# A new hand-written order for the opening of a fused attention and max-out kernel, with one load for the first states

## The chip, the cores and the metric

The kernel runs on one core of one Trainium2 chip. Its metric is the device time of one execution in microseconds; three runs gave 149.94, 150.06 and 150.39 us, so the median is 150.06 us. Lower is better.

## What is computed

Eight batches with eight heads each; x is a sequence of 512 rows of 64, and `state` has 32 rows of 64 for each batch and head. x reads the states by a softmax, the states read x by another, and all rows of both readings, with the heads side by side (512 wide), go through a max-out layer.

```python
scores = scale * x @ state.T          # per batch and head; scale = 1/8
xread  = softmax(scores)  @ state     # 512 rows
sread  = softmax(scores.T) @ x        # 32 rows
rows   = concat([xread, sread])       # (8 * 544) rows of 512
out    = maximum(rows @ w1, rows @ w2) @ w_out     # w1, w2: 512x1024, w_out: 1024x512
```

All inputs and the output are float32 in the chip's main memory.

## The kernel before, in words

**The algebra.** max(h1, h2) is relu(h1 - h2) + h2. So the kernel forms wd = w1 - w2 (512x1024) and wwo = w2 @ w_out (512x512) once, and a batch needs relu(rows @ wd) @ w_out + rows @ wwo. Since xread is a softmax times the state, state @ wd and state @ wwo are made first for each batch (`sw`, 32 rows for each head), and the softmax weights are multiplied with those (`l1` for the relu part, the `o` part of `l2` for the other). The eight heads stand as two groups g of four heads of 32 rows each, 128 rows in all.

**The stages of a batch.** x is loaded as two halves of four heads (512 KB each, `load_x`), cast to bfloat16 (`cast_e` four pieces, `cast_b` two pieces) and transposed: for batches 0 and 1 on TensorE (`xt`, evicted by `xte`), for the others by a transposing DMA (`xtd`). `sc` makes the scores against `sbd`, a tile with the transposed states (two half batches hh), `exp` evicts them on ScalarE, `red` sums and inverts on VectorE, `mul` normalises, and the weights are transposed (`at` on TensorE and its eviction `ate` for batches 0 and 1, `atd` by DMA for the others). `sw` (L331 on, eight products to a token) and its evictions `swe`; `l1` with the evictions `re` (a relu, on ScalarE or VectorE); `l2` with the evictions `le`; then `store`. The other reading, `sr`, is made directly for batches from 2 on; for batches 0 and 1 `srw` makes a wider product, `swre` evicts it into `srx`, and `srp` (`sr_pick`, four copies of 32 partitions each) later picks out the right parts. `srx` lies in the same memory as batch 2's `sw` tile, so `swe.2` waits for the picks.

**The weights.** Each of w1, w2 and w_out comes in four pieces of 512 KB (`ldw1`, `ldw2`, `ldwo`). For w1 and w2, pieces 0 and 1 are the columns 0 to 511 (rows 0 to 255 and 256 to 511) and pieces 2 and 3 the columns 512 to 1023. Each piece of w2 is cast (`cw2`), transposed on TensorE (`w2`) and evicted (`w2e`) for wwo; each piece of w_out is cast (`cwo`); `ww.i.q` adds to row block i of wwo what a quarter q of the 1024 columns gives, and `wwe` evicts it. `sub.k.h` makes half h of piece k of wd from the float32 pieces of w1 and w2. `sw.b.0` and `sw.b.1` need the columns 0 to 511 and 512 to 1023 of wd, `sw.b.w` needs wwo.

**The order.** Batches 0 and 1 and the start of batch 2 run by ORDER, a list of tokens that a loop (L517) emits in turn; every engine does its own tokens in that order, and waits are placed by the tile framework. A token is name.arguments@PSUM banks>engine (A ScalarE, V VectorE, P GpSimd); `fill.k@bank` is a product of zeros on TensorE that nothing reads (512 columns where k is 100 or more, else 256). SyncE issues the loads, transposes and stores in the order of the list. The states come by `ldS.lo.hi` (L178): 0 in ScalarE's DMA queue, 1 and then 2 to 7 in SyncE's; `cS` casts states 0 and 1, `S` transposes them on TensorE, `Se` evicts one half j of the partitions into `sbd`. States 2 to 7 are cast with a mask in two parts (`mS`, L202) and transposed into `sbd` by one DMA (`Sd`, L211).

**The rest.** From batch 2 on a plain loop (L602) does l1 of batch b, scores of b + 1, casts and transposes of b + 2, the load of b + 3, then l2 of b; RELEASE tells in which order its banks come. A sum check (`check_sums`) ends in a product with a column of ones whose result, `flag` (L645, L646), decides whether a general path runs. The last batch and the state rows (`m1`, `m2`) follow. WHOLE names batches whose x comes as one load of 1 MB (L621).

## Time and profile before

| What | Value |
|---|---|
| median of three runs | 150.06 us |
| the profiled execution's own time | 150.39 us |
| span of that execution, first to last instruction | 148.5 us |
| TensorE busy | 138.9 us (94%), 1185 products |
| VectorE, ScalarE, GpSimd busy | 84.7, 67.3, 55.7 us |
| mean granted TensorE clock | 0.996 |
| main memory read, written | 15.20 MB, 8.91 MB |

The profile is of one execution. Times in its rows are microseconds from the first instruction. PE is TensorE (PEld its weight loads), DVE VectorE, ACT ScalarE, POOL GpSimd, SP SyncE; a q behind a name is that engine's sequencer, which issues DMAs. L336 is line 336 of the kernel. Rows of the chain of waits give start, length and what; rows of the timeline give start, length, engine, line, operation, written tile <- read tile, shape and count, and in brackets how long the engine stood idle before it and what ended that. The length of a product on TensorE is that of one product from its start to its modelled end; products overlap, and the chain gives the pace. In rows on DMA issues the last number is the time from issue to landing, in us.

### The profile page before, as it was taken

How to read it: one execution, taken by the hardware profiler on the slowest of the kernel's cores; microseconds unless marked ns; L12 is line 12 of the kernel's file. 1: busy time of each engine (PE TensorE's matmuls, PEld its weight loads, DVE VectorE, ACT ScalarE, POOL GpSimd, SP SyncE). 2: the span in 40 equal slices, each digit the busy share in tenths (PEclk: the TensorE clock that was granted, in tenths of full speed). 3: DMA queues.
4: the chain of work that ended last, by engine and by line, in shares of the span. 5: the costliest groups of instructions: out<-in, count | busy, mean ns of one | idle time of the engine just before them, and what ended most of it. 6: DMA issues, size and time to landing. Idle time of an engine off the chain costs nothing.

```text
span 148.5 us, 3021 instructions
## 1 busy us (share of the span) xinstructions
PE 138.9 (94%) x1185; PEld 69.2 (47%) x1185; DVE 84.7 (57%) x164; ACT 67.3 (45%) x123; POOL 55.7 (38%) x89
## 2 busy tenths in 40 slices
...
GB/s 136 309 376 388 384 387 382 281 281 226 83 203 76 72 185 382 282 187 328 249 93 274 256 181 102 252 306 122 71 71 216 29 44 177 110 0 131 81 160 61
DMA packets 36063, 29.44 MB, mean 198 GB/s; under 512 B 23120, under 2 KB 31568, under 8 KB 35152
## 3 DMA queue, kind: packets, MB, share of 16 engines
...
q8 instruction: 10, 0.16, 0.5%
...
HBM read 15.20 MB, written 8.91 MB: 162 GB/s over the span
## 4 chain that ended last, share of the span: by engine, by line
PE 83%; DMA 11%; SPq 1%; DVE 1%; issue 0%; ACT 0%
PE bank L373 37%; PE bank L359 19%; PE bank L368 10%; DMA big<-in_moe_w_dram 8%; PE bank L336 4%; DMA big<-in_x_dram 3%; PE bank L488 3%; PE bank L392 2%; PE bank L402 2%; PE bank L248 2%; PE bank L288 1%; PE bank L400 1%; DVE wd L444 1%; SPq L175 1%; PE bank L432 1%; SPq L171 0%
## 5 line engine op out<-in xcount | busy, mean ns | idle before, releaser
L373 PE MATMUL bank<-wo,r 128*128 128x512 bf16 (+1 forms) x264 | 60.8, 373 | 0.0
L373 PEld LDWEIGHTS <-r 128*128 128x128 bf16 x264 | 25.5, 98 | 28.9 <-issue 0.2
L354 DVE TENSOR_SCALAR r<-bank 128x512 bf16<-128x512 f32 x30 | 20.7, 691 | 19.5 <-PE bank L359 19.1
L359 PE MATMUL bank<-at,sw 128*128 128x512 bf16 x128 | 30.1, 379 | 0.0
L101 ACT COPY big<-bank 128x512 f32<-128x512 f32 (+1 forms) x17 | 9.7, 573 | 41.3 <-PE bank L373 39.7
L264 POOL TENSOR_TENSOR a<-e,er 128x512 bf16<-128x512 bf16 x15 | 15.9, 1079 | 29.9 <-DVE er L261 15.0
L352 ACT ACTIVATE r<-bank 128x512 bf16<-128x512 f32 x34 | 20.4, 609 | 6.6 <-PE bank L359 6.5
L103 DVE CAST sw<-bank 128x512 bf16<-128x512 f32 x24 | 15.1, 684 | 7.2 <-PE bank L336 6.5
L368 PE MATMUL bank<-sw,at 128*128 128x512 bf16 (+1 forms) x66 | 19.0, 374 | 0.0
L103 DVE COPY big<-bank 128x512 f32<-128x512 f32 (+1 forms) x16 | 10.6, 661 | 14.5 <-PE bank L373 14.5
L359 PEld LDWEIGHTS <-sw 128*128 128x128 bf16 x128 | 12.1, 98 | 13.8 <-DVE sw L103 0.3
L105 POOL CAST xb<-big 128x1024 bf16<-128x1024 f32 x12 | 12.3, 1039 | 15.7 <-DMA big<-in_x_dram 10.8
L105 POOL CAST xe<-big 128x512 bf16<-128x512 f32 x26 | 15.3, 622 | 6.3 <-DMA big<-in_x_dram 6.3
L101 ACT CAST sw<-bank 128x512 bf16<-128x512 f32 x24 | 12.7, 599 | 3.2 <-PE bank L336 3.1
L256 ACT ACTIVATE e<-bank 128x512 bf16<-128x512 f32 x16 | 8.9, 594 | 9.5 <-PE bank L248 9.0
L260 DVE TENSOR_REDUCE sums<-e 128x16 f32<-128x512 bf16 x16 | 10.5, 656 | 3.1 <-ACT e L256 3.0
L488 PE MATMUL bank<-wo,w2m 128*128 128x512 bf16 x32 | 8.1, 379 | 0.4 <-POOL wo L105 0.3
L368 PEld LDWEIGHTS <-at 128*128 128x128 bf16 x66 | 5.5, 98 | 5.0 <-issue 0.2
L454 PE MATMUL bank<-wz 128*128 128x512 bf16 (+1 forms) x18 | 5.5, 422 | 1.3 <-DVE ones L457 1.3
L248 PEld LDWEIGHTS <-xt 128*128 128x128 bf16 x128 | 5.1, 98 | 1.9
L336 PE MATMUL bank<-wd,sbd 64*32 64x512 bf16 x128 | 5.7, 382 | 0.1
L248 PE MATMUL bank<-sbd,xt 128*128 128x64 bf16 x128 | 5.5, 193 | 0.0
...
## 6 DMA issues: line engine op xcount, KB each, us to landing
...
big<-in_moe_w_dram SPq DMA_DIRECT2D x8, 512.0 KB, 11.3
big<-in_moe_w_out_dram SPq DMA_DIRECT2D x4, 512.0 KB, 10.8
...
sf<-in_state_dram SPq DMA_DIRECT2D x1, 384.0 KB, 11.1
```

Source lines behind the costliest of these rows:

```text
L101: nc.scalar.copy(o, i)
L103: nc.vector.tensor_copy(o, i)
L105: nc.gpsimd.tensor_copy(o, i)
L248: nc.tensor.matmul(pv[:, c, kk], xt_s[b % 2][:, c, k, :], sbd[:, b, k, :], start=(c == 0 and kk == 0), stop=(c == NC - 1 and kk == 1))
L264: (nc.gpsimd if eng == "P" else nc.vector).tensor_mul(e_view(a_s[b % 2], hh), e_view(e_s[b % 2], hh), er_s[b % 2][:, hh].unsqueeze(3).to_b ...
L336: nc.tensor.matmul(pg[g][32 * i:32 * i + 32, 0:n], sbd[64 * g:64 * g + 64, b, i, 32 * g:32 * g + 32], rhs, start=True, stop=True)
L352: nc.scalar.activation(out=o, in_=p, func=ACTF.Relu)
L354: nc.vector.tensor_scalar(o, p, scalar1=0.0, scalar2=None, op0=ALU.max)
L359: nc.tensor.matmul(p, sw_s[b % 3][:, g, f * 128:(f + 1) * 128], at_s[b % 3][:, g].rearrange("p c t -> p (c t)"), start=(g == 0), stop=(g = ...
L368: nc.tensor.matmul(p[:, lo:hi], at_s[b % 3][:, g, c, :], sw_s[b % 3][:, g, FF + lo:FF + hi], start=(start and g == 0), stop=(stop and g == 1))
L373: nc.tensor.matmul(p[:, lo:hi], r_s[b % 2][:, f, c * 128:(c + 1) * 128], wo[:, f, lo:hi], start=(start and j == 0), stop=(stop and j == le ...
L488: nc.tensor.matmul(p, w2t[:, f, i, :], wo[:, f, :], start=(first and f % 2 == 0), stop=(last and f % 2 == 1))
```

## The change

It replaces ORDER, with the same work in it but for the fills (27 in place of 18) and the states: one load `ldS.0.2` in ScalarE's queue brings states 0 and 1, two neighbouring rows of a state to a partition (pieces of 512 bytes in place of 256), `cS.0.2` casts both, `S.0.2` transposes both, and `Se` makes two copies, each of which puts the row pairs back in order. The list has other weight pieces first (columns 512 to 1023 ahead of columns 0 to 511), another choice of engine for several evictions and casts, both `mS` on ScalarE, both halves of batch 2's x ahead of the load of states 2 to 7, and `srp` ahead of `mul.2.0` where it stood behind both `mul.2`. RELEASE changes. x of batch 7 comes in two loads. The product of `flag` has 128 columns of ones (`full`, set by GpSimd behind the list) where it had two. `gate` is defined and the new list doesn't call it. The old list is shown down to its first l1, the new one in full.

```diff
--- before.py
+++ after.py
@@ -21,37 +21,37 @@
 ORDER = """
-ldx.0.0 ldS.0.1 fill.113@0 ldx.0.1 fill.104@1 ldS.1.2 fill.112@0 ldx.1.1 fill.111@1 ldx.1.0 fill.108@0 fill.13@1
-ldw2.0 fill.109@0 ldw2.1 fill.115@1 fill.105@0 ldwo.0 ce.0.0>V ce.0.1>A fill.11@1 ldw1.1 cS.0.1>V xt.0.0@1 ldwo.1
-S.0.1@0 ldw1.0 fill.0@2 ce.0.2>V ce.0.3>A ldw2.3 Se.0.1.0>V cS.1.2>P Se.0.1.1>V xte.0.0>A xt.0.1@2 ldw2.2 fill.15@0
-S.1.2@3 xte.0.1>V Se.1.2.1>A sc.0.0@1 ldwo.3 ce.1.2>P Se.1.2.0>A fill.102@0 sc.0.1@2 exp.0.0>A fill.2@0 fill.12@3
-ce.1.3>V ldwo.2 exp.0.1>A red.0.0>V xt.1.1@1 srw.0@2,3 ce.1.0>A ce.1.1>P red.0.1>V ldw1.2 mul.0.0>P xte.1.1>A xt.1.0@0
-swre.0.1>V mul.0.1>P cw2.0>A ldw1.3 xte.1.0>V swre.0.0>V cw2.1>P at.0.0@0 sc.1.0@2 ldx.3.1 w2.0@3 ate.0.0>V exp.1.0>A
-fill.114@0 sc.1.1@1 w2e.0>V cwo.0>P w2.1@0 exp.1.1>A at.0.1@2 red.1.0>V w2e.1>A ww.1.0@1 srw.1@3,4 red.1.1>V sub.1.1>P
-ldS.2.8 ww.3.0@0 mul.1.1>V cwo.1>A fill.1@5 fill.3@6 ww.2.0@7 sub.1.0>V swre.1.0>A ww.0.1@6 sub.0.0>V swre.1.1>A
-ww.1.1@1 ww.3.1@0 sub.0.1>V ww.0.0@6 ate.0.1>V mul.1.0>P sw.0.0@4,3 sw.1.0@2,5 swe.0.0.1>A swe.0.0.0>V ww.2.1@7
-cw2.3>P swe.1.0.1>A at.1.1@3 swe.1.0.0>V l1.0.2@4 at.1.0@5 ate.1.1>V cw2.2>P w2.3@2 re.0.2>A ate.1.0>V l1.0.3@3
...
+ldx.0.0 ldS.0.2 fill.10@0 ldx.0.1 fill.109@1 ldx.1.1 fill.114@0 fill.11@1 ldx.1.0 fill.110@0 ldw2.2 fill.100@1
+fill.9@0 ldw2.3 fill.111@1 ldwo.2 fill.0@0 fill.5@1 fill.101@0 ldw1.3 ce.0.1>A ce.0.0>V ldwo.3 xt.0.0@0 cS.0.2>V
+ldw1.2 fill.106@1 xte.0.0>V fill.105@2 ce.0.3>P ce.0.2>A ldw2.1 S.0.2@1 xt.0.1@2 ldw2.0 Se.0.2.1>A Se.0.2.0>V sc.0.0@1
+xte.0.1>V fill.13@0 ldwo.0 fill.6@3 ce.1.2>P exp.0.0>A fill.115@4 fill.108@3 sc.0.1@4 ce.1.3>V ldwo.1 red.0.0>V
+exp.0.1>A xt.1.1@3 ce.1.0>A ce.1.1>P srw.0@4,1 xte.1.1>V ldw1.0 mul.0.0>P swre.0.0>A red.0.1>V sc.1.1@3 xt.1.0@2
+cw2.2>P exp.1.1>A ldw1.1 fill.15@4 fill.107@0 xte.1.0>V fill.1@4 swre.0.1>A fill.2@3 fill.14@0 fill.3@4 fill.112@3
+cw2.3>A red.1.1>V mul.0.1>P fill.102@4 fill.7@3 ldx.2.0 fill.4@2 mul.1.1>V w2.3@2 cwo.2>A w2.2@3 w2e.3>V sc.1.0@4
+at.0.0@0 at.0.1@1 exp.1.0>A w2e.2>V ww.3.2@2 ldx.2.1 ww.2.2@4 red.1.0>V sub.3.1>P ate.0.0>A srw.1@3,5 ate.0.1>A
+mul.1.0>V cwo.3>A ww.0.2@1 sub.3.0>V at.1.0@0 at.1.1@6 swre.1.0>A ww.1.2@7 sub.2.0>V ate.1.1>A ldS.2.8 ww.3.3@2
+ww.1.3@7 sub.2.1>V ate.1.0>A ww.0.3@1 swre.1.1>A sw.1.1@0,6 sw.0.1@5,3 swe.1.1.0>A swe.1.1.1>V ww.2.3@4 swe.0.1.0>A
+swe.0.1.1>V l1.1.5@6 cw2.1>P l1.1.7@0 cw2.0>A re.1.5>V l1.0.7@3 w2.1@5 re.1.7>V re.0.7>A w2.0@6 w2e.1>V cwo.0>A
+l1.0.5@3 l1.1.6@0 w2e.0>V l1.1.4@5 cwo.1>A ww.2.0@4 re.0.5>V ww.1.0@7 re.1.4>A ww.2.1@4 sub.0.0>V ww.1.1@7 re.1.6>A
+sub.0.1>V ww.3.0@2 wwe.2>A ww.0.1@1 sub.1.1>V ww.3.1@2 wwe.1>A ww.0.0@1 sub.1.0>V wwe.3>A l1.0.4@7 wwe.0>A cb.2.0>P
+sw.0.0@2,4 re.0.4>V sw.1.0@0,5 swe.0.0.1>A sw.0.w@1,3 swe.1.0.1>V sw.1.w@7,6 ce.2.0>P swe.1.0.0>A l2.1.3.3@4
+swe.1.w.0>V cb.2.1>P l2.1.2.3@5 swe.0.0.0>A l2.1.2.2@5 swe.1.w.1>V swe.0.w.1>A l1.1.2@2 ce.2.3>P xtd.2 mS.1>A
+swe.0.w.0>V l2.1.3.2@4 ce.2.1>P l1.0.3@3 l1.0.1@1 re.1.2>A ce.2.2>P l1.1.0@6 re.0.3>A re.0.1>V l2.0.2.2@2 l1.0.6@7
+re.1.0>V mS.0>A l1.1.3@1 l1.0.2@6 re.0.6>A Sd l2.0.3.o@3 ldx.4.1 re.0.2>A l2.1.3.o@4 ldx.3.0 l2.0.3.3@3 re.1.3>A
+l1.0.0@6 ldx.4.0 l1.1.1@1 re.0.0>V l2.1.0.o@7 ldx.3.1 l2.1.0.2@7 re.1.1>V l2.0.0.1@6 l2.1.2.0@5 l2.1.0.0@7 l2.1.2.o@5
+l2.0.0.o@6 sc.2.0@1 l2.0.3.1@3 exp.2.0>A l2.1.1.3@0 l2.0.2.o@2 red.2.0>V l2.1.3.1@4 l2.1.3.0@4 srp.0>P srp.1>P
+mul.2.0>P l2.1.1.1@0 le.1.3>A sc.2.1@1 l2.1.1.2@0 ce.3.0>P exp.2.1>A l2.1.0.1@7 ce.3.1>P l2.0.2.3@2 red.2.1>V
+l2.1.2.1@5 cb.3.0>P l2.0.3.0@3 le.1.2>V l2.0.0.3@6 mul.2.1>P l2.1.1.0@0 l2.0.0.2@6 l2.1.1.o@0 ce.3.3>P atd.2
+l2.1.0.3@7 ce.3.2>P le.1.1>A l2.0.3.2@3 le.1.0>V l2.0.0.0@6 cb.3.1>P le.0.3>A sr.2@0 le.0.0>V sw.2.0@3,7 xtd.3
+sw.2.w@5,1 sre.2>V swe.2.0.0>A sw.2.1@6,4 l2.0.2.0@2 swe.2.w.1>A swe.2.w.0>V l2.0.1.3@0 swe.2.1.1>A l2.0.2.1@2
+swe.2.0.1>V l2.0.1.o@0 le.0.2>A l2.0.1.2@0 swe.2.1.0>A l2.0.1.0@0 srt.2@2 l2.0.1.1@0 srte.2>A le.0.1>V store.0
 """
 
 LATE = 2
 
-WHOLE = (7,)
-
-RELEASE = [5, 1, 3, 0, 7, 2, 6, 4]
+WHOLE = ()
+
+RELEASE = [3, 1, 5, 4, 7, 6, 2, 0]
 
 
 @with_exitstack
@@ -137,6 +137,7 @@
     r_s = many(2, "r", [NF, NC * 128])
     wb_s = many(2, "wb", [1024])
     big = many(10, "big", [2048], F32)
+    gt, = many(1, "gt", [1])
     srd = wz.bitcast(F32).rearrange("p (b z) -> p b z", b=2)
     srx = sw_s[2].rearrange("p g w -> p (g w)")[:, 0:2080].bitcast(F32).rearrange("p (b g k z) -> p b g k z", b=2, g=2, k=4)
 
@@ -176,6 +177,11 @@
                           in_=moe_w_out[256 * q:256 * q + 256, :].rearrange("(f p) n -> p f n", p=128))
 
     def load_s(lo, hi):
+        if hi <= LATE:
+            (nc.scalar if lo == 0 else nc.sync).dma_start(
+                out=sf[:, lo:hi].rearrange("p b g d -> p b (g d)"),
+                in_=state[lo:hi].rearrange("b h (n m) d -> (h n) b (m d)", m=2))
+            return
         (nc.scalar if lo == 0 else nc.sync).dma_start(
             out=sf[:, lo:hi].rearrange("p b g d -> p (b g) d"),
             in_=state[lo:hi].rearrange("b (g i) n d -> (i n) (b g) d", g=2))
@@ -196,8 +202,11 @@
         return p
 
     def s_ev(p, lo, hi, j, eng):
-        copy(eng, sbd[64 * j:64 * j + 64, lo:hi, :, 32 * j:32 * j + 32],
-             p[64 * j:64 * j + 64, 0:(hi - lo) * 256].rearrange("p (b k z n) -> p z b k n", k=4, z=2, n=Ns)[:, j])
+
+        for b in range(lo, hi):
+            copy(eng, sbd[64 * j:64 * j + 64, b, :, 32 * j:32 * j + 32].rearrange("p k (n m) -> p k n m", m=2),
+                 p[64 * j:64 * j + 64, 256 * (b - lo):256 * (b - lo) + 256].rearrange(
+                     "p (m k z n) -> p z k n m", m=2, k=4, z=2)[:, j])
 
     def s_mask(z, lo, hi, eng):
         o = sb[:, lo:hi].rearrange("p b g z d -> p (b g) z d")[:, :, z, :]
@@ -443,6 +452,11 @@
         hf, o = lo // 512, lo // 512 * 512
         (nc.gpsimd if eng == "P" else nc.vector).tensor_sub(
             wd[:, i0:i1, lo:hi], half(1, hf)[:, i0:i1, lo - o:hi - o], half(2, hf)[:, i0:i1, lo - o:hi - o])
+
+
+    def gate(k, h, eng):
+        lo, hi, i0, i1 = piece(k, h)
+        copy(eng, gt, wd[:, i1 - 1, hi - 1:hi])
 
     def wo_cast(q, eng):
         copy(eng, wo[:, 2 * q:2 * q + 2, :], half("o", q // 2)[:, q % 2 * 2:q % 2 * 2 + 2, :])
@@ -506,7 +520,7 @@
         xte=("xt", xt_ev), exp=("sc", lambda p, b, h, e: sc_ev(p, b, h)), ate=("at", at_ev),
         sre=("sr", lambda p, b, e: sr_ev(p, b)), srte=("srt", sr_cp), re=("l1", l1_ev), w2e=("w2", w2_ev))
     oth = dict(
-        swre=lambda b, g, e: srw_ev(done[f"srw.{b}"], b, g, e), srp=sr_pick,
+        swre=lambda b, g, e: srw_ev(done[f"srw.{b}"], b, g, e), srp=sr_pick, gate=gate,
         ldS=load_s, ldx=load_x, ldp=load_p, ldw2=lambda k: load_w(2, moe_w2, k), ldw1=lambda k: load_w(1, moe_w1, k), ldwo=load_wo,
         idle=idle, fill=lambda k, r: idle(1, r, 512 if k >= 100 else 256, k >= 200), cS=s_cast, mS=lambda z, e: s_mask(z, LATE, B, e), Sd=lambda: s_dma(LATE, B), ce=cast_e, cb=cast_b, xtd=xt_dma,
         atd=at_dma, red=lambda b, h, e: red(b, h), mul=mul, cw2=w2_cast, sub=w_sub, cwo=wo_cast, ww=ww_mm, l2=l2_mm,
@@ -537,6 +551,8 @@
     e2 = wb_s[0][0:64, 0:512]
     cl, ne = (w.bitcast(F32)[:, 0:B * 34] for w in wb_s)
     bad, = many(1, "bad", [1])
+    full, = many(1, "full", [128])
+    nc.gpsimd.memset(full, 1.0)
     flag, = many(1, "flag", [1], I32)
     dl = big[3][:, 0:512]
 
@@ -642,7 +658,7 @@
         sr_cp(sr_tr(n, "r"), n, "A")
         if n == B - 1:
             p = bank("r")
-            nc.tensor.matmul(p[0:2, 0:1], ones, bad, start=True, stop=True)
+            nc.tensor.matmul(p[:, 0:1], full, bad, start=True, stop=True)
             nc.vector.tensor_copy(flag[0:1, :], p[0:1, 0:1])
         store(b)
```

14 lines of the change are left out of this document (removed).

## The prediction

> **What bounds the kernel now.** I read the busy time by stage first, then the chain of waits, then the single rows of the opening. The first view cuts the span where the chain stops waiting; its columns are the stretch, its length, busy time (and instructions) of TensorE, its weight loads, VectorE, ScalarE and GpSimd, the granted clock, the DMA share and GB/s.
>
> ```profile
> span 148.5 us, 3021 instructions
> 0.00:20.49 20.49, 15.17 (x142) 9.14 (x143) 13.49 (x28) 11.30 (x18) 10.28 (x30) 1.00 0.93 325
> 20.49:144.26 123.77, 123.72 (x1043) 60.05 (x1042) 71.22 (x137) 55.60 (x105) 45.46 (x60) 1.00 0.66 181
> ```
>
> From 20.49 on TensorE is busy 123.72 of 123.77 us: the rest of the kernel is a fixed amount of matrix work without a hole. Only the time that TensorE wastes ahead of 20.49 (idle, or in fills, which compute nothing) can be won, and any new wait behind it is lost in full. The chain of waits (start, length, what) tells what ends the opening:
>
> ```profile
> 7.80 11.32 DMA big<-in_moe_w_dram
> ...
> 19.15 1.30 DVE wd L444 x2
> ...
> 20.49 0.74 PE bank L336 x14
> 21.24 0.54 PE bank L488 x2
> ...
> 22.68 0.45 PE bank L432 x8
> ...
> 45.16 0.23 PE bank L248 x8
> ```
>
> The sixth weight load (w1.0) lands at 19.12, VectorE makes two differences (sub), then sw.0.0 runs and TensorE never waits again. The chain also gives what saturated work costs: eight transposes 0.45, eight score products 0.23, two 512-column products 0.43 (0.54 behind an sw group), an sw product 0.05 (14 in 0.74; each sw token has eight).
>
> **Wasted time before.** Ahead of 20.49 ORDER does 60 transposes (32 xt, 4 S, 8 at, 16 w2): 3.38. Then 32 score products: 0.94; 14 ww products: 14 x 0.216 = 3.02; 16 srw products of 260 columns: 16 x 0.216 x 260/512 = 1.75; the first two of sw.0.0: 0.1. Together 9.19, so 20.49 - 9.19 = 11.30 us are wasted.
>
> **The loads.** Each row below is an instruction that began when a load landed (start, length, engine, what, what ended the idle time).
>
> ```profile
> 4.49 0.62 ACT L101 CAST xe<-big 128x512 bf16<-128x512 f32 x1 [2.18 <-DMA big<-in_x_dram]
> 6.27 0.62 ACT L101 CAST xe<-big 128x512 bf16<-128x512 f32 x1 [1.16 <-DMA big<-in_x_dram]
> 7.45 0.40 POOL L105 CAST sb<-sf 128x256 bf16<-128x256 f32 x1 [5.12 <-DMA sf<-in_state_dram]
> 8.85 0.87 POOL L105 CAST xe<-big 128x512 bf16<-128x512 f32 x1 [1.01 <-DMA big<-in_x_dram]
> 10.35 0.61 POOL L105 CAST xe<-big 128x512 bf16<-128x512 f32 x1 [0.62 <-DMA big<-in_x_dram]
> 13.05 1.04 POOL L105 CAST wb<-big 128x1024 bf16<-128x1024 f32 x1
> 14.40 1.04 POOL L105 CAST wo<-big 128x1024 bf16<-128x1024 f32 x1 [0.32 <-DMA big<-in_moe_w_out_dram]
> 17.10 1.04 ACT L101 CAST wo<-big 128x1024 bf16<-128x1024 f32 x1 [0.99 <-DMA big<-in_moe_w_out_dram]
> 20.43 1.04 POOL L105 CAST wb<-big 128x1024 bf16<-128x1024 f32 x1 [1.92 <-DMA big<-in_moe_w_dram]
> q8 instruction: 1, 0.02, 5.9%
> ```
>
> A half of x costs 1.50 (8.85 to 10.35), a weight piece 1.35 (13.05 to 14.40). State 0, in ScalarE's queue, cost 6.27 - 4.49 - 1.50 = 0.28; state 1, in SyncE's, 8.85 - 6.27 - 1.50 = 1.08. From 17.10 to 20.43 two pieces took 3.33 instead of 2.70; in 16.9 to 18.1 an instruction packet held one of the 16 DMA engines for 5.9% of 16 x 1.2 = 1.1 us (the last row). TensorE had then issued its first 256 instructions or so, a weight load with each product; ORDER brings it there again, at ww.3.2, so I keep that 0.6.
>
> The merged load moves 128 KB in as many pieces as one old load (256, of 512 B): 0.28 if pieces count, 0.56 if bytes do; I take 0.4, since an x half shows that both count. State 1's 1.08 goes. So everything from x1.1 on lands 0.95 earlier; I use 0.9. The bounds are 1.08 (nothing added) and -0.28 (the 1.08 belonged to something else and the bytes come on top). By the Trainium skill, "DMA: Bandwidth & Descriptors", section "Issuing engines are not separate DMA queues", another issuing engine saves issue time only, as the same 16 engines carry the bytes; by that rule the loads would hardly move, and the trace, with 0.28 against 1.08 for the same bytes, does not agree.
>
> **The new opening.** Durations:
>
> ```profile
> 9.28 0.69 DVE L260 TENSOR_REDUCE sums<-e 128x16 f32<-128x512 bf16 x1
> 10.00 0.25 DVE L261 RECIPROCAL er<-sums 128x16 f32<-128x16 f32 x1
> 11.74 1.05 ACT L101 CAST wb<-big 128x1024 bf16<-128x1024 f32 x1
> 13.71 0.60 ACT L256 ACTIVATE e<-bank 128x512 bf16<-128x512 f32 x1 [0.92 <-PE bank L248]
> 16.59 1.01 DVE L264 TENSOR_TENSOR a<-e,er 128x512 bf16<-128x512 bf16 x1
> 17.02 1.50 POOL L264 TENSOR_TENSOR a<-e,er 128x512 bf16<-128x512 bf16 x1
> 17.53 1.53 DVE L444 TENSOR_TENSOR wd<-big,big 128x512 bf16<-128x512 f32 x1
> ```
>
> The first pieces become w2.2, w2.3, wo2, w1.3, wo3, w1.2, in the places of w2.0, w2.1, wo0, w1.1, wo1, w1.0: they land at 10.8, 12.15, 13.5, 14.9, 16.2 (16.8 with the instruction packet) and 18.2. ScalarE casts w2.3 to 13.2. TensorE has then done xt 1.80, S 0.23, sc 0.70, srw.0 0.88: 3.61, and wasted 9.59. The 27 fills (18 before) lie inside that wait: eleven ahead of xt.0.0, ten between xt.1.0 (over at 11.3) and w2.3, at most 1.5 of work in 1.9.
>
> From 13.2 I walk its list: w2.3 to 13.65, w2.2 14.1, sc.1.0 14.35, at.0.0 and at.0.1 14.85, ww.3.2 and ww.2.2 15.7, srw.1 16.6, ww.0.2 17.0. Beside it ScalarE casts wo2 (13.5 to 14.55) and does exp.1.0 (to 15.15); VectorE does red.1.0 (0.9) to 16.1 and mul.1.0 (1.01) to 17.1, so at.1.0 waits 0.1. Then at.1.0, at.1.1 and four ww (0.45 and 1.73) end at 19.3; cwo.3 (16.8 to 17.85) is in time for ww.3.3 at 18.1. w1.2 at 18.2 plus two subs (1.30, chain) gives 19.5, where sw.1.1 gets going in earnest. Each later gate has a lead: ww.2.0 at 24.3 against cwo.0 at 23.95; l1.0.4, behind two sw 0.85, nine ww 3.9, six l1 2.6 and two w2 0.9, at 27.8 against w1.1 (26.3) plus two subs, 27.6. At 19.5 the work done is 3.83 for 68 transposes (two at groups more than before), 0.94, 1.75, 3.02 and 0.1: 9.64. Wasted: 9.86, that is the 9.59 and 0.3 of waits behind it. I add 0.2 for hand-overs of banks between 20 and 33, where ScalarE has leads of 0.1 to 0.3: 10.06. Gain: 11.30 - 10.06 = 1.24.
>
> Small edits of the opening: the states' evictions read PSUM with another stride, the same four copies of 64x128 (at 0.45 a pair before), hidden, since sc.0.0 waits for xt.0.1 anyway; doubled, they would show 0.2. ScalarE takes the at copies from VectorE, 128x512 each: bounded by 0.37 for 260 columns and 0.60 for 512 in other forms; I took 0.55, hidden.
>
> **Behind the opening.**
>
> ```profile
> 19.14 1.89 SPq L179 DMA_DIRECT2D sf<-in_state_dram  x1
> sf<-in_state_dram SPq DMA_DIRECT2D x1, 384.0 KB, 11.1
> 31.92 0.96 ACT L206 ACTIVATE sb<-sf,mask 128x768 bf16<-128x768 f32 x1
> 33.11 2.56 SPq L212 DMA_TRANSPOSE sbd<-sb  x1
> sbd<-sb SPq DMA_TRANSPOSE x1, 6.5
> xt<-xb SPq DMA_TRANSPOSE x1, 4.3
> 109.39 3.45 PE bank L359 x16
> ...
> 123.33 3.56 PE bank L359 x16
> 49.30 2.62 POOL L105 COPY wz<-sw 32x130 f32<-32x130 f32 x8
> ```
>
> States 2 to 7 landed at 19.14 + 11.1 = 30.2. Now they follow both halves of x2: w1.1 26.3, x2.0 27.8, x2.1 29.3, states 30.9 (1.6 for them: 1.1 by bytes as an x half, 1.7 by 1536 pieces at state 0's 0.28 for 256). Both masks stand in ScalarE's queue (one was GpSimd's, 2.21 off its path), at 31.0 and 33.0, with re.1.2, re.0.3 and so l2.0.2.2 behind the first; re.1.2 ends at 32.6, and TensorE, with 13.8 of work from 19.5, gets to l2.0.2.2 at 33.3. The transposed load Sd follows xtd.2 in SyncE's queue, goes at 34.0 and lands between 38.3 (the 4.3 of another transpose with an empty queue) and 40.5 (its own 6.5, with loads ahead of it; ldx.4.1 and the x3 halves now stand behind). sc.2.0 needs it; ahead of it TensorE has, from 19.5, 48 sw products 2.5, nine ww 3.9, sixteen l1 6.9, two w2 0.9 and fifteen l2 6.5: 20.7, and comes at 40.2. I take 38.3, as those loads are gone: no wait; at 40.5 it is 0.3.
>
> The picks run from about 32 on an idle GpSimd, ahead of mul.2.0: their 2.62 leave the end of the list, where TensorE did not wait either: nothing. Splitting x7 adds one SyncE issue (about 0.5) near 91, while SyncE has nothing else to do: nothing. The wide flag product: the l1 group behind it took 3.56 against 3.45, and I expect that 0.11 to go (bounds 0 and 0.2, its own 0.09 included). `full` costs one memset behind the list; `gate` isn't called. New RELEASE: nothing, each bank of the first l1 is out of ORDER before.
>
> **Sum.** 1.24 + 0.11 = 1.35. The profiled execution took 150.39 (1.9 around its span of 148.5), so 149.04; it was the highest of the three, and on their median the forecast is 150.06 - 1.35 = **148.7**.
>
> **Rivals.** (1) The loads don't come earlier, which the bounds allow: the bytes are the same. (This is what the rule of the Trainium skill named above would make of it.) Then w1.2 is at 19.12, sw.1.1 goes at 20.42 with 9.60 done: 10.8 wasted, 11.0 with hand-overs. The new list alone gains 0.3, with the flag 0.4, and 0.7 if a third of the shift comes: 149.4 to 149.7. Against it: 1.08 beside 0.28 for the same bytes.
>
> (2) VectorE becomes the bound from 8 to 19: without a hole in my walk. GpSimd's mul took 1.50 and VectorE's sub 1.53 beside each other at 17.0 to 19.1, where VectorE's own mul took 1.01 and a sub of the chain 0.65. Now mul.1.1 on VectorE meets mul.0.1 on GpSimd, and mul.1.0 meets the end of sub.3.1. Two such meetings at 0.4 shift VectorE by 0.8; 0.2 of it lies in the wait for w1.2, so sw.1.1 goes 0.6 later: 149.3. The Trainium skill, "SBUF — State Buffer", section "SBUF: two separate sides", has GpSimd and a VectorE operation with two SBUF inputs lock each other out for a whole instruction; those two rows agree.
>
> (3) The same time: tight hand-overs on ScalarE from 20 to 33 and Sd at 40.5 cost 1.0 and 0.3 more: 150.0.
>
> (4) Slower: the first mask. If states 2 to 7 land late, ScalarE stands at its first mask, its relus behind it, and Sd goes as much later. With Sd's 6.5, each us behind 30.9 is one on TensorE, past the 0.3. It turns the sign at 1.35 - 0.3 = 1.05 late, and passes 0.3% at 1.5 late. At 3 late (the load now queues behind 1 MB of x2): 150.06 - 1.35 + 3.3 = 152.0.
>
> **Chances.** 0.3% (0.45 us) is about what a measurement of this kernel tells from no change. Forecast 0.54 (148.1 to 149.2), rival 1 0.14, rival 2 0.12, rival 3 0.09, rival 4 0.11. Half of rival 1 is faster by over 0.3%, half is not; rival 3 is the same time: faster 0.73, same 0.16, slower 0.11. The range runs from 147.9 (loads 1.08 earlier, 0.2; no hand-over waits, 0.2; 0.2 at the flag; the instruction packet behind w1.2, 0.2 until TensorE's own list binds) to 150.0, which leaves out rival 4 and half of rival 3.
>
> **What would show it.** Right: x1.1's casts begin near 7.9, w2.3's near 12.2, and from about 13.2 the stage table shows TensorE full; the first sw near 19.4; sc.2 near 40, not waiting for sbd; the l1 behind the flag at 3.45. Wrong: casts of x1.1 still at 8.8 (rival 1); long VectorE and GpSimd products side by side (2); TensorE idle by relus between 20 and 33 (3); ScalarE idle until sf lands, or sc.2 released by sbd (4).

## The result, and the profile after

The changed kernel takes **149.69 us** (median of 16 executions, 149.50 to 150.26) against 150.11 us for the kernel before on the same chip (16 executions): a ratio of 0.9968, 95% interval 0.9958 to 0.9979. It is faster by 0.42 us, or 0.3%. The forecast was a gain of 1.35 us, so its direction was right and more than two thirds of its size did not come. The two profiled executions lie further apart than the medians, since that of before (150.39) was a long one: 150.39 against 149.55.

Busy time by stage, changed kernel, columns as before the change, cut at 20.25 (the sw group runs), at 53.52 (the hand-written order ends) and behind TensorE's last work. A last row takes out 13.80 to 20.25.

```profile
span 147.7 us, 3018 instructions
0.00:20.25 20.25, 17.61 (x157) 11.24 (x160) 13.57 (x27) 12.26 (x22) 8.07 (x27) 1.00 0.92 323
20.25:53.52 33.27, 32.78 (x265) 15.37 (x269) 18.57 (x33) 20.16 (x35) 15.93 (x26) 1.00 0.80 219
53.52:143.60 90.08, 89.45 (x758) 44.28 (x768) 52.47 (x103) 37.46 (x73) 25.46 (x32) 1.00 0.60 169
13.80:20.25 6.45, 6.23 (x63) 4.11 (x65) 5.17 (x9) 5.16 (x9) 1.27 (x1) 1.00 1.05 385
```

The shape is the forecast one: TensorE is full from 13.80 on (6.23 of 6.45), and it stays nearly full. But the boundary that the forecast put at 19.5, where the sw group gets going, is at 20.4. The chain of waits of the changed kernel (start, length, what):

```profile
6.39 11.29 DMA big<-in_moe_w_out_dram
17.70 1.05 ACT wo L101
18.80 1.46 PE bank L502 x6
...
21.72 1.46 PE bank L368 x6
...
53.52 3.45 PE bank L368 x16
```

It now passes through a piece of w_out (wo3, cast from 17.70) where it passed through w1.0 before. The timeline says when each load was taken up and what TensorE did then:

```profile
6.39 0.62 ACT L101 CAST xe<-big 128x512 bf16<-128x512 f32 x1 [1.31 <-DMA big<-in_x_dram]
8.49 1.04 POOL L105 CAST xe<-big 128x512 bf16<-128x512 f32 x1 [1.38 <-DMA big<-in_x_dram]
12.71 1.04 ACT L101 CAST wb<-big 128x1024 bf16<-128x1024 f32 x1 [0.33 <-DMA big<-in_moe_w_dram]
13.80 1.07 PE L441 MATMUL bank<-ident,wb 128*128 128x128 bf16 x16 [0.47 <-ACT wb L101]
14.02 1.04 ACT L101 CAST wo<-big 128x1024 bf16<-128x1024 f32 x1 [0.27 <-DMA big<-in_moe_w_out_dram]
17.70 1.04 ACT L101 CAST wo<-big 128x1024 bf16<-128x1024 f32 x1 [1.00 <-DMA big<-in_moe_w_out_dram]
19.05 1.29 DVE L453 TENSOR_TENSOR wd<-big,big 128x512 bf16<-128x512 f32 x2 [0.98 <-DMA big<-in_moe_w_dram]
20.18 0.84 PE L345 MATMUL bank<-wd,sbd 64*32 64x512 bf16 x16
20.98 0.69 DVE L103 CAST sw<-bank 128x512 bf16<-128x512 f32 x1 [0.64 <-PE bank L345]
21.72 1.02 PE L368 MATMUL bank<-at,sw 128*128 128x512 bf16 x4 [0.17 <-DVE sw L103]
q8 instruction: 1, 0.02, 5.9%
```

The row of the sw group at 20.18 merges two starts. A window that begins at 20.58 leaves out the group's first two products and shows where the other 14 start:

```profile
20.40 0.62 PE L345 MATMUL bank<-wd,sbd 64*32 64x512 bf16 x14
```

That is when the second difference of w1.2 is done (19.05 + 1.29 = 20.34). Before the change these 14 products started at 20.49.

The reader is to see three things. The second half of batch 1's x is taken up at 8.49 (8.85 before, 7.9 by the forecast). The sixth weight piece, w1.2, starts its two differences at 19.05, where before the sixth piece started them at 19.15; the forecast had 18.2. And behind the sw group the first l1 (21.72) waits for VectorE's eviction of sw. The last row is the instruction packet in the 1.2 us from 15.4. By the trace's times it begins at 15.42 (16.94 before); wo3 then lands at 17.68, 2.34 behind w1.3, where a piece costs 1.35.

### The profile page after: what moved, and what is told of

It reads as the page before. It is cut to its first block, busy times and chain, and to the rows that moved or that the text cites. A ratio compares the mean times of both kernels' runs of the same rounds, so it can differ in the third digit from the quotient of the medians.

```text
span 147.7 us, 3018 instructions
## 1 busy us (share of the span) xinstructions
PE 139.9 (95%) x1176; PEld 70.9 (48%) x1194; DVE 84.6 (57%) x162; ACT 70.3 (48%) x129; POOL 49.5 (34%) x85
## 4 chain that ended last, share of the span: by engine, by line
PE 83%; DMA 11%; ACT 1%; issue 1%; DVE 0%; SPq 0%; DVEq 0%
PE bank L382 38%; PE bank L368 19%; PE bank L377 9%; DMA big<-in_moe_w_out_dram 8%; PE bank L345 4%; DMA big<-in_x_dram 3%; PE bank L502 3%; PE bank L401 2%; PE bank L411 2%; PE bank L257 2%; PE bank L297 1%; PE bank L409 1%; ACT wo L101 1%; PE bank L441 1%; DVE sw L103 0%
## 5 line engine op out<-in xcount | busy, mean ns | idle before, releaser
L363 DVE TENSOR_SCALAR r<-bank 128x512 bf16<-128x512 f32 x32 | 21.8, 690 | 18.2 <-PE bank L368 17.7
L101 ACT COPY big<-bank 128x512 f32<-128x512 f32 (+1 forms) x16 | 9.2, 573 | 44.4 <-PE bank L382 39.7
L273 POOL TENSOR_TENSOR a<-e,er 128x512 bf16<-128x512 bf16 x14 | 14.5, 1050 | 33.0 <-DVE er L270 23.4
L361 ACT ACTIVATE r<-bank 128x512 bf16<-128x512 f32 x32 | 19.4, 612 | 5.1 <-PE bank L368 4.8
L103 DVE COPY big<-bank 128x512 f32<-128x512 f32 (+1 forms) x17 | 11.2, 661 | 13.0 <-PE bank L382 13.0
L103 DVE CAST sw<-bank 128x512 bf16<-128x512 f32 x23 | 14.5, 683 | 6.7 <-PE bank L345 6.7
L105 POOL CAST xe<-big 128x512 bf16<-128x512 f32 x27 | 16.1, 632 | 5.9 <-DMA big<-in_x_dram 5.9
L377 PE MATMUL bank<-sw,at 128*128 128x512 bf16 (+1 forms) x56 | 16.8, 372 | 0.3
L468 PE MATMUL bank<-wz 128*128 128x256 bf16 (+1 forms) x26 | 7.2, 428 | 1.3 <-DVE ones L471 1.3
L103 DVE COPY w2m<-bank 128x1024 bf16<-128x1024 bf16 (+1 forms) x5 | 3.3, 687 | 4.3 <-PE bank L411 4.1
```

The lines of the kernel that those rows point to most:

```text
L101: nc.scalar.copy(o, i)
L103: nc.vector.tensor_copy(o, i)
L105: nc.gpsimd.tensor_copy(o, i)
L273: (nc.gpsimd if eng == "P" else nc.vector).tensor_mul(e_view(a_s[b % 2], hh), e_view(e_s[b % 2], hh), er_s[b % 2][:, hh].unsqueeze(3).to_b ...
L361: nc.scalar.activation(out=o, in_=p, func=ACTF.Relu)
L363: nc.vector.tensor_scalar(o, p, scalar1=0.0, scalar2=None, op0=ALU.max)
```

## The experiments

A table first, since the landings of the weight pieces explain most of it: one profiled execution of each, "sixth" being w1.0 in the old list and w1.2 in the new, us from the first instruction. "sw" is the start of the first sw group.

| kernel | packet begins | fifth lands | sixth lands | seventh lands | sw | time, median | ratio, 95% interval |
|---|---|---|---|---|---|---|---|
| before | 16.94 | 17.07 | 19.12 | 20.31 | 20.49 | 150.11 | |
| after | 15.42 | 17.68 | 19.03 | 20.38 | 20.40 | 149.69 | 0.9968 [0.9958, 0.9979] |
| merged_alone | 16.46 | 16.57 | 19.22 | 20.57 | 20.59 | 150.26 | 1.0006 [0.9993, 1.0018] |
| state1_in_sync | 15.89 | 16.25 | 19.08 | 20.43 | 20.45 | 150.21 | 1.0001 [0.9973, 1.0029] |
| state1_again | 16.04 | 16.36 | 19.15 | 20.51 | 20.53 | 150.25 (one) | |
| weight_third | 18.03 | 17.62 | 20.21 | 21.56 | 23.66 | 152.9 (one) | |
| late_packet | 17.75 | 16.65 | 18.00 | 20.44 | 20.02 | 149.38 | 0.9948 [0.9929, 0.9968] |
| late_warm | 18.04 | 17.14 | 18.50 | 20.31 | 20.25 | 149.41 | 0.9968 [0.9947, 0.9990] |
| before_late | 18.03 | 17.43 | 20.30 | 21.65 | 21.67 | 151.18 | 1.0062 [1.0035, 1.0088] |
| late_ww | 17.56 | 16.75 | 19.71 | 20.99 | 21.08 | 149.47 (this one 150.40) | 0.9949 [0.9934, 0.9964] |
| ww_moved | 15.13 | 17.64 | 19.00 | 20.35 | 20.37 | 149.76 | 0.9985 [0.9973, 0.9998] |
| few_ww | 17.55 | 16.33 | 17.70 | 20.32 | 19.23 | **149.05** | 0.9923 [0.9899, 0.9947] |

(Where the first two products of a group start ahead of the rest and wait again, "sw" is the start of the rest. Each ratio is against the kernel before, run on the same chip at the same time; its median there was 150.09 to 150.21, so medians of two rows can differ by 0.1 for that alone.) My theory after the result was that the loads' head start was small at x1.1 to begin with, and that the instruction packet, which the new list calls earlier, then took it away. The rivals were that state 1's own load is what had been slow, and that something other than loads (cold products, hand-overs of banks) keeps TensorE.

### Does the merged load bring anything? (merged_alone)

The kernel before with only the load, cast, transposes and evictions of states 0 and 1 changed as in the new kernel.

```diff
-ldx.0.0 ldS.0.1 fill.113@0 ldx.0.1 fill.104@1 ldS.1.2 fill.112@0 ldx.1.1 fill.111@1
+ldx.0.0 ldS.0.2 fill.113@0 ldx.0.1 fill.104@1 fill.112@0 ldx.1.1 fill.111@1
...
-S.0.1@0 ldw1.0 fill.0@2 ce.0.2>V ce.0.3>A ldw2.3 Se.0.1.0>V cS.1.2>P Se.0.1.1>V
+S.0.2@0 ldw1.0 fill.0@2 ce.0.2>V ce.0.3>A ldw2.3 Se.0.2.0>V Se.0.2.1>V
```

> The old kernel with the merged load of states 0 and 1 as its only change (one load in ScalarE's queue, 512-byte pieces; one cast, one S, two Se on VectorE). Theory A: most of the 2.56 us between x0.1 and x1.1 is a hole in the transfers that has nothing to do with state 1, so x1.1's casts come near 8.45 (before 8.83), every weight piece 0.3 to 0.4 earlier, and the time falls by about 0.3 us. Theory B (the prediction's): state 1's place in SyncE's queue cost 1.08, so x1.1's casts come near 7.9 and the time falls by about 0.9.

x1.1 landed at 8.31, 0.49 earlier than in the kernel before, and the pieces up to the fifth kept it (16.57 against 17.07). Then the packet came at 16.46, and the sixth piece landed at 19.22, 2.65 behind the fifth: no gain, 150.26. The first theory had the loads right, but the 0.3 that it gave the time did not come. So the merged load is worth half of what the prediction gave it, and a head start of 0.5 at the fifth piece was worth nothing at the sixth.

### Was state 1 itself the slow load? (state1_in_sync, state1_again, weight_third)

The changed kernel with state 1 back in SyncE's queue as a load of its own, in pieces of 512 bytes; the second run is the same kernel once more.

```diff
-ldx.0.0 ldS.0.2 fill.10@0 ldx.0.1 fill.109@1 ldx.1.1 fill.114@0
+ldx.0.0 ldS.0.1 fill.10@0 ldx.0.1 fill.109@1 ldS.1.2 ldx.1.1 fill.114@0
```

> The changed kernel with its load of states cut in two: state 0 in ScalarE's queue, state 1 in SyncE's behind x0.1, where it stood before, both with 512-byte pieces. Theory A: only the order of the bytes changes, x1.1's casts stay between 8.4 and 8.6. Theory B: the place in SyncE's queue costs 0.7 or more by itself, x1.1's casts come at 9.1 or later. State 1 lands at about 7 instead of 4.9 in both, so the cast of the states, and the first scores behind it, come later, up to 0.4 us on the time.

> The same kernel as state1_in_sync, for a second look at its transfers (x1.1 landed there 1.46 behind state 1, with no hole). If that order of loads is what removes the hole: x1.1's casts near 8.0 again. If the hole comes and goes from run to run: casts anywhere between 8.0 and 8.6. In both w1.2 lands near 19.

```profile
6.18 0.62 ACT L101 CAST xe<-big 128x512 bf16<-128x512 f32 x1 [1.13 <-DMA big<-in_x_dram]
6.49 0.68 DVE L103 CAST sb<-sf 128x512 bf16<-128x512 f32 x1 [1.63 <-DMA sf<-in_state_dram]
7.88 0.61 POOL L105 CAST xe<-big 128x512 bf16<-128x512 f32 x1 [0.99 <-DMA big<-in_x_dram]
```

These timeline rows of state1_again give x0.1, states and x1.1. State 1 as third load of SyncE's queue costs about 0.23 here (landings 6.16 and 6.39; 0.22 in the first run), and x1.1 lands at 7.83 and 7.97, **earlier** than with the merged load (8.02 to 8.60 in its eight profiles). Both theories of the first run missed that; the first of the second run, that this order of loads has no such gap, held. The 1.08 that I had read as state 1's price is not the price of its 64 KB nor of its queue. Its pieces of 256 bytes may have a part in it: the three profiles with the old loads show 1.08, 0.75 (flag_alone) and 1.49 (before_late). No run changes the size of the pieces alone.

At the sixth piece nothing of that is left: it landed at 19.08 and 19.15, a packet having come at 15.9 to 16.0, and the hand-written order ended at 53.57 and 53.65, close to the changed kernel's 53.52. That the time is 0.5 above the changed kernel's all the same does not come from the opening. The last product ends at 143.73 and 143.80, in the changed kernel at 143.68, but the execution goes on for another 4.7 and 4.6 us in place of 4.0. What makes the end longer here stays open.

In the changed kernel x1.1 itself is the third load of SyncE's queue and lands 2.07 behind x0.1, where 1.50 was its price. Does that extra go with the load or with the place? Here a weight piece stands there:

```diff
-ldx.0.0 ldS.0.2 fill.10@0 ldx.0.1 fill.109@1 ldx.1.1 fill.114@0 fill.11@1 ldx.1.0 fill.110@0 ldw2.2 fill.100@1
+ldx.0.0 ldS.0.2 fill.10@0 ldx.0.1 fill.109@1 ldw2.2 ldx.1.1 fill.114@0 fill.11@1 ldx.1.0 fill.110@0 fill.100@1
```

> The changed kernel with w2.2 as the third load of SyncE's queue, ahead of both x1 halves. If the hole of 0.6 belongs to the third load or to that time: w2.2 lands near 8.3 (1.9 behind x0.1 instead of 1.35) and x1.1 1.5 behind it. If it belongs to x1.1: w2.2 lands at 7.75 and x1.1 2.0 behind it. The time is 0.5 to 1.5 higher, as batch 1 starts a piece later.

w2.2 landed at 9.25, 2.84 behind x0.1 where a piece costs 1.35, and x1.1 then took 1.45. So the extra is not x1.1's; it goes with the third place (or that time), and was longer here. It is a gap in the transfers: from 5.50 to 6.75 the DMA engines move 267 GB/s in the changed kernel and 334 in state1_in_sync, which has no extra. The 152.9 of this kernel says nothing about it: batch 1's x came 2.3 later.

### Is it the packet? (late_packet, late_warm, before_late)

The packet came with TensorE's 128th product or so, and the warm-up products count. The first kernel keeps 9 of the 27 and has none ahead of xt.0.0:

```diff
-ldx.0.0 ldS.0.2 fill.10@0 ldx.0.1 fill.109@1 ldx.1.1 fill.114@0 fill.11@1 ldx.1.0 fill.110@0 ldw2.2 fill.100@1
-fill.9@0 ldw2.3 fill.111@1 ldwo.2 fill.0@0 fill.5@1 fill.101@0 ldw1.3 ce.0.1>A ce.0.0>V ldwo.3 xt.0.0@0 cS.0.2>V
+ldx.0.0 ldS.0.2 ldx.0.1 ldx.1.1 ldx.1.0 ldw2.2 ldw2.3 ldwo.2 ldw1.3 ce.0.1>A ce.0.0>V ldwo.3 xt.0.0@0 cS.0.2>V
...
-cw2.2>P exp.1.1>A ldw1.1 fill.15@4 fill.107@0 xte.1.0>V fill.1@4 swre.0.1>A fill.2@3 fill.14@0 fill.3@4 fill.112@3
-cw2.3>A red.1.1>V mul.0.1>P fill.102@4 fill.7@3 ldx.2.0 fill.4@2 mul.1.1>V w2.3@2
+cw2.2>P exp.1.1>A ldw1.1 fill.107@0 xte.1.0>V swre.0.1>A fill.112@3 fill.101@4 fill.103@3
+cw2.3>A red.1.1>V mul.0.1>P fill.102@4 ldx.2.0 mul.1.1>V w2.3@2
```

> The changed kernel with 9 fills instead of 27, so that TensorE's 256th instruction comes 18 products later, near the end of the at products of batch 1 at about 18 us. Theory P: the instruction packet held up wo3 by 1.0; now wo3 lands at 16.7 (changed kernel 17.68) and w1.2 at 18.05 (19.03), sw.1.1 starts near 19.5 (20.18), and the time falls by 0.5 to 0.7 below the changed kernel's, to about 149.1. Rival: wo3 is late for another reason and stays at 17.7, no gain; or without the fills the array slows down and the first products take twice as long, which costs 0.3 or more.

The packet moved to 17.75, the fifth and sixth piece landed at 16.65 and 18.00 with no delay, and the delay (2.44 in place of 1.35) fell on the seventh, which nothing waits for there. 149.38, 0.31 below the changed kernel, where I expected 0.5 to 0.7; the intervals of the two ratios overlap a little (0.9958 to 0.9968). The fills that are gone were not in the way themselves: in the changed kernel TensorE stood idle for 0.47 behind the last of them, until w2.3 was cast. The chain of waits of late_packet:

```profile
12.97 0.95 ACT wb L99
13.97 1.07 PE bank L439 x16
...
18.37 1.73 PE bank L500 x8
21.37 1.46 PE bank L366 x6
...
53.16 3.45 PE bank L366 x16
```

From 13.97 (w2.3's cast is over) to the sw group at 20.02 TensorE alone makes the chain: w1.2 is 2 us ahead of its use. The next bound is TensorE's own list from 13.97 and the wait at 21.37. The order ends at 53.16 in place of 53.52: 0.36 for the packet, from one profile of each kernel. (flag_undone, below, has the changed kernel's opening and ends its order at 53.69, so such an end moves by 0.17 of itself.)

The second kernel keeps 9 too, but eight wide ones ahead of xt.0.0 and one behind it, so that the early products aren't slow ("cold"):

```diff
-fill.9@0 ldw2.3 fill.111@1 ldwo.2 fill.0@0 fill.5@1 fill.101@0 ldw1.3 ce.0.1>A ce.0.0>V ldwo.3 xt.0.0@0 cS.0.2>V
+ldw2.3 fill.111@1 ldwo.2 fill.101@0 fill.112@1 fill.113@0 ldw1.3 ce.0.1>A ce.0.0>V ldwo.3 xt.0.0@0 cS.0.2>V
...
-cw2.2>P exp.1.1>A ldw1.1 fill.15@4 fill.107@0 xte.1.0>V fill.1@4 swre.0.1>A fill.2@3 fill.14@0 fill.3@4 fill.112@3
+cw2.2>P exp.1.1>A ldw1.1 xte.1.0>V swre.0.1>A
```

> The changed kernel with 9 fills again, but eight wide ones ahead of xt.0.0 and one behind it, and none between xt.1.0 and w2.3. Theory P with warmth: the instruction packet stays late (wo3 near 16.7, w1.2 near 18.0, the next piece takes 2.4), and the transposes and scores of 5 to 10 us run at full pace again (eight xt products in 0.45 to 0.6, in late_packet 1.03), so w2.3's transposes start near 13.8 and the time is that of late_packet or up to 0.3 lower. Rival: the fills between xt.1.0 and w2.3 are what keeps the pace up; without them the w2 transposes run at half pace, and the time is 0.3 higher.

149.41 with 148.94 to 150.46 over 12 executions. The second group of xt transposes took 0.62 as in the changed kernel, in late_packet 1.06, but that is worth nothing that can be told from late_packet. So cold products are not the cause. In the profiled execution x1.1 came late (8.60), the packet still missed w1.2, and the order ended at 53.40, only 0.12 before the changed kernel's. Over all executions its ratio is the changed kernel's own, 0.9968. So this kernel alone doesn't show a gain by the late packet.

The third is the kernel before, all 18 warm-up products dropped and nothing else:

```diff
-ldx.0.0 ldS.0.1 fill.113@0 ldx.0.1 fill.104@1 ldS.1.2 fill.112@0 ldx.1.1 fill.111@1 ldx.1.0 fill.108@0 fill.13@1
+ldx.0.0 ldS.0.1 ldx.0.1 ldS.1.2 ldx.1.1 ldx.1.0
...
-ldS.2.8 ww.3.0@0 mul.1.1>V cwo.1>A fill.1@5 fill.3@6 ww.2.0@7 sub.1.0>V
+ldS.2.8 ww.3.0@0 mul.1.1>V cwo.1>A ww.2.0@7 sub.1.0>V
```

> The kernel before with its 18 warm-up products gone and nothing else changed: old list, old state loads, old flag product. Theory P (the packet's place decides): the packet comes about 3 us later than at 16.94, behind the landing of w1.0 and w1.2, which come at 18.3 to 18.6 in place of 19.12; the tensor work that waits for them starts some 0.5 earlier, and the time is 149.5 to 149.8. Theory L (the new list and its order of pieces are what the packet's move pays with, and the old list has other waits ahead): w1.0 lands earlier but the products of the opening run cold and behind their casts, 150.0 to 150.4. If the old list gains as much as the new one did from a late packet (0.3), the change itself keeps its own 0.4; if it gains nothing, a late packet is of use to the new list alone.

My expectation for the packet missed: it came only 1.1 later, at 18.03, with 113 products begun, and so in the middle of w1.0's flight instead of behind it. Timeline of before_late, w1.0's differences:

```profile
20.32 1.29 DVE L442 TENSOR_TENSOR wd<-big,big 128x512 bf16<-128x512 f32 x2 [0.75 <-DMA big<-in_moe_w_dram]
21.67 0.74 PE L334 MATMUL bank<-wd,sbd 64*32 64x512 bf16 x14 [0.21 <-DVE wd L442]
```

w1.0 lands at 20.30, 2.87 behind the fifth piece, the sw group starts 1.2 later than before the change, and the kernel is 0.6% slower. The profiled execution was a long one (152.19, the median is 151.18). This fits the same mechanism in the other direction, but the run doesn't separate it from the cold products that this list then has, so it can't say what the new list is worth by itself.

### Is it the hand-over behind sw? (late_ww, ww_moved, few_ww)

ww.0.3 (four products) moves from ahead of sw.1.1 to behind sw.0.1, so that TensorE has work while VectorE evicts sw; first on top of late_packet.

```diff
-ww.1.3@7 sub.2.1>V ate.1.0>A ww.0.3@1 swre.1.1>A sw.1.1@0,6 sw.0.1@5,3
+ww.1.3@7 sub.2.1>V ate.1.0>A swre.1.1>A sw.1.1@0,6 sw.0.1@5,3 ww.0.3@1
```

> The kernel of late_packet (changed kernel with 9 fills) with ww.0.3 moved from ahead of sw.1.1 to behind sw.0.1. Theory H: behind the two sw TensorE waits for the evictions swe with only ww.2.3 (0.43) to do, from about 21.0 to 21.37 in late_packet, while sw.1.1 could have started 0.4 earlier; with ww.0.3 in the gap the wait goes, and the time falls by 0.3 to 0.4 below late_packet's 149.38. Rival: sw.1.1 is gated by its banks or by the last sub at 20.0 in any case, the wait only moves ahead of it, no change.

The wait at the first l1 went, but in the profiled execution the packet (17.56) caught w1.2 (19.71, 2.96 behind the fifth piece), the sw group started at 21.08, and that execution took 150.40. The other five took 148.93 to 149.76. The same program, packet in or behind w1.2's flight, spreads over 1.5 us. That is an argument from one profile; the others weren't profiled.

Then the same move alone in the changed kernel, its 27 warm-up products kept:

> The changed kernel with one product of its list moved: ww.0.3 (four products, 0.86 us) from ahead of sw.1.1 to behind sw.0.1, all 27 warm-up products kept. Theory H (in the changed kernel 0.3 us are lost at the hand-over from sw.0.1 to l1.1.5, where only ww.2.3 lies behind the two sw groups and VectorE's first eviction of sw takes longer than that): no wait of l1.1.5 for DVE or ACT, the end of the hand-written order 0.2 to 0.35 earlier, 149.3 to 149.5. Theory D (sw.1.1 waits for the wd tile of sub.2.0 and sub.2.1, which the sixth weight piece sets, so that moving work away from ahead of it only turns the later wait into an earlier one): sw.1.1 waits up to 0.5 at 19.3 to 20.3 and the time stays at 149.6 to 149.75.

```profile
18.99 0.98 ACT at L101 x2
20.01 0.98 PE bank L345 x16
20.99 0.97 PE bank L502 x4
21.96 1.29 PE bank L368 x6
...
53.60 3.45 PE bank L368 x16
```

In this chain of waits l1 follows the moved product directly (20.99 + 0.97 = 21.96), but the time comes back ahead of sw: the group's first two products start at 20.01, where 20.18 less the 0.86 that was moved would be 19.32, and the other 14 at 20.37, when the second difference of w1.2 is done (20.32). The first two waited for ScalarE's eviction of `at`, which stands behind the cast of wo3 (17.67): so the late fifth piece holds them too. The order ends at 53.60 against 53.52, and the time is 149.76: no gain, as the second theory said. So the wait that the trace of the changed kernel shows behind sw is no loss of its own as long as the sixth piece comes at 19.0; it is the same wait in another place.

Last, both with fewer warm-up products still (three kept):

```diff
-ldx.0.0 ldS.0.2 fill.10@0 ldx.0.1 fill.109@1 ldx.1.1 fill.114@0 fill.11@1 ldx.1.0 fill.110@0 ldw2.2 fill.100@1
-fill.9@0 ldw2.3 fill.111@1 ldwo.2 fill.0@0 fill.5@1 fill.101@0 ldw1.3 ce.0.1>A ce.0.0>V ldwo.3 xt.0.0@0 cS.0.2>V
+ldx.0.0 ldS.0.2 ldx.0.1 ldx.1.1 ldx.1.0 ldw2.2 ldw2.3 ldwo.2 ldw1.3 ce.0.1>A ce.0.0>V ldwo.3 xt.0.0@0 cS.0.2>V
...
-ww.1.3@7 sub.2.1>V ate.1.0>A ww.0.3@1 swre.1.1>A sw.1.1@0,6 sw.0.1@5,3
+ww.1.3@7 sub.2.1>V ate.1.0>A swre.1.1>A sw.1.1@0,6 sw.0.1@5,3 ww.0.3@1
```

> The changed kernel with 24 of its 27 warm-up products gone (three are left: one 512 wide behind the sixth weight piece's issue, one ahead of sc.0.1, one behind the issue of w1.1), and with ww.0.3 moved from ahead of sw.1.1 to behind sw.0.1. The instruction packet comes with TensorE's 128th product, so it moves behind the sixth weight piece for good. Theory P (the packet's place among the weight pieces set what the loads' shift was worth, and the hand-over behind sw.0.1 took the rest): packet after 18.2, w1.2 lands at 18.0 to 18.5, sw.1.1 starts by 20.1, l1.1.5 follows the moved product without a wait for DVE or ACT, and the time is 148.7 to 149.2 with no execution near 150.4. Theory W (the warm-up is needed, and the list's gain was its own): the early products run cold, sw.1.1 starts after 20.3, time 149.5 to 150.0. Theory N (the loads' landings converge behind the packet, so an earlier w1.2 changes only which wait is last): sw.1.1 at 19.6 to 20.0 but 149.4 as in the run with 18 fewer warm-up products.

**149.05 us**, 148.81 to 149.59: below both kernels, 1.1 under before and 0.6 under the change. It is the one kernel of the series that is faster than the changed one with the two intervals apart. Timeline of few_ww:

```profile
17.21 1.89 DVE L451 TENSOR_TENSOR wd<-big,big 128x512 bf16<-128x512 f32 x3
19.23 0.63 PE L343 MATMUL bank<-wd,sbd 64*32 64x512 bf16 x16
20.66 1.46 PE L366 MATMUL bank<-at,sw 128*128 128x512 bf16 x6
21.75 1.05 ACT L99 CAST wb<-big 128x1024 bf16<-128x1024 f32 x1 [0.94 <-DMA big<-in_moe_w_dram]
```

The three differences run on end from 17.21, sw starts at 19.23 and l1 at 20.66, neither waiting. By its chain of waits the order ends at 52.95, against 53.16 in late_packet:

```profile
52.95 3.45 PE bank L366 x16
```

The first l1 starts 0.71 before that of late_packet (21.37). Of this 0.36 is an earlier start of w2.3's transposes (13.61 for 13.97), which leaves 0.35 for the move of ww.0.3: with the sixth piece early, it pays. Of the 0.71 only 0.21 is left at the end of the order, since the chain now runs through the eighth piece, taken up at 21.75. Here too the packet came earlier than I expected, at 17.55 and not behind 18.2: it missed w1.2 by little.

### The wide flag product (flag_alone, flag_undone)

```diff
+    full, = many(1, "full", [128])
+    nc.gpsimd.memset(full, 1.0)
...
-            nc.tensor.matmul(p[0:2, 0:1], ones, bad, start=True, stop=True)
+            nc.tensor.matmul(p[:, 0:1], full, bad, start=True, stop=True)
```

flag_alone puts this into the kernel before; flag_undone takes it out of the changed one.

> The old kernel with the flag product 128 columns wide as its only change. Theory A: the flag product and the l1 group behind it take 3.47 together, as in the changed kernel (before 0.09 and 3.56), and the time falls by 0.1 to 0.2 us. Rival: the l1 group was long for another reason, both stay 3.65, no change of time.

> The changed kernel with the flag product of before in place of the wide one: a stationary of 128x2 ones in place of 128x128, and the flag read from two partitions. If the wide product is worth what the two profiles show (0.18), the time is 0.1 to 0.25 above the changed kernel's 149.69, so 149.8 to 149.95, and the wait between the flag product and the next l1 returns at about 0.09 with 3.56 for the group. If that row was only a difference of two executions, the time is within 0.1 of 149.69 and the group takes 3.47 to 3.50.

flag_alone took 150.28, ratio 0.9993 [0.9970, 1.0016]: no difference that can be told, with the sixth piece at 19.69 in its profiled execution. flag_undone took 149.78, 0.9974 [0.9962, 0.9985], 0.09 above the changed kernel, which the intervals don't separate either. The traces do. The chain of waits at the flag and the l1 behind it, changed kernel first, then flag_undone:

```profile
122.86 0.00 PE bank L661
122.87 3.47 PE bank L368 x16
```

```profile
123.04 0.09 PE bank L659
123.14 3.56 PE bank L368 x16
```

The narrow product costs 0.09 and the group behind it 0.09 more, as before the change (0.09 and 3.56). That is 0.18 in three pairs of profiles (flag_alone had 0.00 and 3.48).

## Why the prediction was wrong in size

**What the gain is made of.** In the profiled executions the order ends at 53.52 in place of 53.89: 0.37. The row of before's chain of waits that answers to the 53.52 above:

```profile
53.89 3.24 PE bank L359 x15
```

The flag product gives 0.18. The spans differ by 0.83; the other 0.28 lies behind the last product, in the last store, which took 2.87 from issue to landing before and 2.59 after. It takes 2.6 to 2.9 in the other profiles, whatever the kernel, so that is no gain of the change. The 0.37 is a reading of one profile each as well: the old opening once more, in flag_alone, ended its order at 54.45, the new one, in flag_undone, at 53.69.

**The step that failed: "everything from x1.1 on lands 0.95 earlier; I use 0.9".** It had two parts.

- *State 1's 1.08.* I read the extra behind x0.1 as the price of state 1. It was the interval in which state 1 landed. With no load there x1.1 still took 2.07 instead of 1.50, and with state 1 there in larger pieces the extra was 0.22. Of the 0.9, x1.1 got 0.36 (8.80 to 8.44), in merged_alone 0.49. (One execution can be off by some 0.3: x1.1 lands at 8.54 to 9.12 in the three profiles with the old loads, and at 8.02 to 8.60 in the eight with the merged one.) What the merged load itself costs was right: 4.44 to 4.87 is 0.43, forecast 0.4. The prediction's bound of "-0.28 (the 1.08 belonged to something else and the bytes come on top)" had named this case; I chose by the nearest row, and a row of before can't say what an interval would have been without its load.
- *The packet's 0.6.* The place was right (ww.3.2, 15.42), the price was not: wo3 came 2.34 behind w1.3, so 1.0. With 0.38 of head start at w1.3 (15.34 for 15.72) and 0.29 more lost behind it than before, w1.2 landed 0.09 earlier than the sixth piece before. From there on the loads came when they had come before: the seventh piece at 20.38 (20.31), the twelfth at 27.23 (27.13; 26.3 in the forecast). That few_ww, with w1.2 at 17.70, is clearly faster, and late_packet, with 18.00, by 0.31, shows that this is what held the opening back. The errors against the forecast, 0.44 at w1.3 (15.34 for 14.9), 0.44 more at wo3 (2.34 for 1.9) and 0.05 won at w1.2, make the 0.83 by which w1.2 missed 18.2.

**What it did to the walk.** w2.3's transposes started at 13.80 for 13.2, cwo.3 ran at 17.70 for 16.8 (TensorE waited 0.17 for it), the differences at 19.05 for 18.2, and the sw group got going at 20.40 for 19.5. Rival 1 had sw.1.1 at 20.42 and 149.4 to 149.7 for just this case, w1.2 at 19.12; the measured 20.40 and 149.69 are its numbers. Its premise was only half true, since x1.1 did come earlier and the packet took it back. The rule of the Trainium skill that I had weighed against the trace, "DMA: Bandwidth & Descriptors", section "Issuing engines are not separate DMA queues", by which moving a load to another engine's queue would hardly move the loads, agrees better with these runs than my reading: state 1 in SyncE's queue had x1.1 at 7.83 and 7.97 and the sixth piece at 19.15 and 19.08, in ScalarE's 8.44 and 19.03, so the move to ScalarE's queue brought the loads no gain.

**Of the 1.24 for the opening**, 0.37 came and 0.87 is missing. By the profiles 0.36 of that is the packet (late_packet; late_warm gives 0.12). The other 0.51 is close to the late start, as late_packet's chain of waits has it: from w2.3's transposes on TensorE alone makes the chain; they begin at 13.97 for 13.2, and the sw group at 20.02 for 19.5. w2.3 landed at 12.58 there, forecast 12.15, and its cast began only at 12.86, behind an eviction on ScalarE. That split is worked out, not tried. The hand-over behind sw is no part of it, since the forecast had taken off 0.2 for that.

**What held.** TensorE was full from w2.3's transposes on, but for 0.22 up to the sw group. VectorE did not become the bound (rival 2): its own sub on the way took 0.68, GpSimd's 1.27. Rivals 3 and 4 did not come: states, masks, Sd and picks, in the timeline of the changed kernel:

```profile
31.66 0.94 ACT L215 ACTIVATE sb<-sf,mask 128x768 bf16<-128x768 f32 x1
33.00 2.62 POOL L105 COPY wz<-sw 32x130 f32<-32x130 f32 x8
33.67 0.93 ACT L215 ACTIVATE sb<-sf,mask 128x768 bf16<-128x768 f32 x1
34.62 1.43 SPq L221 DMA_TRANSPOSE sbd<-sb  x1
40.74 0.40 PE L257 MATMUL bank<-sbd,xt 128*128 128x64 bf16 x8
```

Sd lands at 38.33. That the forecast had 38.3 is luck: it was issued 0.6 later (34.62 for 34.0) and took 0.6 less (3.7 for 4.3). The bound of 6.5 was not needed, and the scores of batch 2 start at 40.74 without a wait. The picks run beside other work. The flag product gave 0.18 for 0.11, within its bounds of 0 and 0.2.
